# A long convolution feeding a two-layer block: channels in the array's stationary operand in the last transform step, and turns by VectorE in blocks of 32

## The chip, the cores and the metric

The kernel runs on one core of one Trainium2 chip. The metric is the device time of one execution in microseconds. The kernel before has a median of 3762.23 us over 3 runs (3761.11 to 3762.27). Traces and profile pages come from one profiled execution each. Engines are named as the profile names them: PE (TensorE matmul), PEld (its weight load), DVE (VectorE), ACT (ScalarE), POOL (GpSimd), and SP (SyncE), which issues almost all DMAs.

## What is computed

Two blocks, one after the other, in float32. The first is a convolution over the sequence by a filter that a small network makes; the second is applied to every row of its output.

```python
# batch 4, seq 12480, d_model 128
h_filt = (relu(pos_emb @ w1) @ w2) * exp(-0.01 * pos)     # (12480, 128)
u = x * v                                                  # (4, 12480, 128)
y = irfft(rfft(u, n=2*S) * rfft(h_filt, n=2*S))[:, :S, :]  # causal convolution by channel
a = (x * y).reshape(4 * 12480, 128)
h = a @ w_in                                               # w_in (128, 2048)
out = (h * cos(h)) @ w_out                                 # w_out (2048, 128)
```

## The kernel before

**The convolution** is a transform over 96 x 120 points in two steps forward and two back, all as matmuls. A position of the sequence is n1 x 120 + n2, with n1 from 0 to 103 (R = 104) and n2 from 0 to 119. The steps of one batch, with their lines:

- `u_units` loads x and v, multiplies them and forms sums and differences of mirrored rows in the big tile `slots` (`u_sums`, L401).
- `f1` (L407): for each channel, a stationary operand of 124 places of one channel, and a moving table of 192 columns. DVE and ACT take turns at moving the results into `parts`, which is a view of `slots` (`f1_evict`).
- `f2` (L448): for each pair of frequencies, a moving operand of all 128 channels. Its result is multiplied with the filter's transform `h`, which is loaded for each unit (`before` in `f2_units`, with `w`), in `f2_product` (DVE, then POOL L474).
- `i1` (L479): for each channel, a stationary operand of 96 places of one channel and a moving table of 120 columns; `i1_evict` (ACT L487, DVE L489) puts the result into `slots`.
- `i2` (L504), the last transform step: for each group g of four rows n2 (`n2s(g)`; 30 groups in a batch), eight matmuls. Stationary is a table `t` of 96 x 104, moving are the 128 channels of one place, so that the result has n1 on the partitions and the channels in the free dimension. `i2_out` multiplies by x (tile `xs`, one DMA a group by `load_pairs`, L376) into `zs` (L511) and stores `zs` to the DRAM tile `zd` (L517).

float32 matmuls run as two passes, so each matmul in the program is two in the profile.

`slots` is laid out as 64 pairs of channels, then places, then the 2 channels of a pair:

```python
slots = spool.tile([P, CB, 2 * N2, 2], F32, name="slots")
```

A channel's places are thus 8 bytes apart, and the channels of one place are 64 runs of 8 bytes.

**The layers** work on tiles of 128 rows of `zd` (the first has 104, the last 88; 98 in all), and every row holds the four n2 of its group, so a tile has up to 512 tokens. `moe_load` loads a tile, `moe_turn` turns it by four PE transposes (helper line L126) into PSUM, from where ACT copies it (L737) to `at`, with the channels on the partitions. Then 16 steps follow, one for each 128 hidden channels: `moe_up` (PE L743, ACT L746, DVE L749, POOL L752), `moe_act` (ACT L757, DVE L759) and, four steps later (`LAG`), `moe_down` (PE L768), which sums into the PSUM bank `acc`. There is one such bank; after the last convolution every second tile uses one of the convolution's banks instead. `moe_evict` (ACT L774) copies the sums, `moe_back` turns them back by four PE transposes and an ACT copy (L783), and `moe_store` (L794) writes them with one DMA for each piece of a group that lies in the tile, about two a tile.

**The order of the work** is written out by hand; no scheduler moves anything. The first batch's convolution runs almost alone; from its last transform step on, the layers' steps and the convolution of the next batches are interleaved: each layer step owes one unit, and `next(conv, ...)` runs pieces of the convolution that are worth it (`I2_STEPS` and its like). Every engine executes its instructions in this order, SP its DMAs too. DMAs count their completion on eight semaphores in turn, so a DMA may wait for the one eight before it. When the convolutions are done, only the layers run. `load(n + 2)` is called at step 12 of tile n.

Of the kernel before, what the change touches and what calls it, by code (L numbers as in the profile page):

```python
# [16 lines left out]
P = 128  # L17
# [13 lines left out]
def kernel(  # L31
# [74 lines left out]
    LAG = 4  # L106
    WCOL = 256

    dram = ctx.enter_context(tc.tile_pool(name="dram", bufs=1, space=DRAM))
    hd = dram.tile([N1 // 2, N2, 2, CB, 4], F32, name="hd")  # L110
    zd = dram.tile([NROWS, G, D], F32, name="zd")
# [241 lines left out]
    def filter_out(pool, bank, aT, slots, j, w2_sb):  # L353

        ps = bank()
        for i, jj in enumerate((j, H - 1 - j)):
            nc.tensor.matmul(ps[0:FR, i * 2 * D:(i + 1) * 2 * D], aT[:, jj, 0:FR],
                             w2_sb[:, :], start=True, stop=True)
        above = pool.tile([FR, 2, CB, 2], F32, name="above", bufs=2)
        pj = ps[0:FR, :].rearrange("p (n b i) -> p n b i", n=4, i=2)  # L360
        nc.scalar.copy(out=above[:, :, :, :], in_=pj[:, 2:4])
        a = H - 2 - 2 * j
        for place, op in ((a, ALU.add), (ODD + a, ALU.subtract)):
            nc.vector.tensor_tensor(
                slots[0:FR, :, place:place + 2, :].transpose([0, 2, 1, 3]),
                pj[:, 1::-1], above[:, :, :, :], op=op)
# [14 lines left out]
    def clear_gap(u):  # L381

        nc.gpsimd.memset(u[:, :, H:ODD, :], 0.0)
# [13 lines left out]
    def u_sums(u, tiles, a):  # L397
        both = tiles[0][:, :, :].rearrange("p h (n b i) -> p h n b i", n=UA, i=2)
        below, above = both[:, 0, ::-1, :, :], both[:, 1, :, :, :]
        for place, op, e in ((a, ALU.add, nc.gpsimd), (ODD + a, ALU.subtract, nc.vector)):  # L400
            e.tensor_tensor(u[0:R, :, place:place + UA, :].transpose([0, 2, 1, 3]),  # L401
                            below, above, op=op)


    def f1_mm(ps, u, b, i):

        nc.tensor.matmul(ps[0:KE, i * 2 * N1:(i + 1) * 2 * N1], u[:, b, 0:KE, i],  # L407
# [12 lines left out]
    def f1_evict(ps, b, share):  # L420
        copy, negated = f1_takers(b, share)
        pj = ps[:, 0:4 * N1].rearrange("p (i r k) -> p r k i", i=2, r=2)
        copy(out=parts[0:ODD, :, :, b, :], in_=pj[0:ODD])
        yield
        copy(out=parts[ODD:KE, 0, :, b, :], in_=pj[ODD:KE, 1])
        negated(parts[ODD:KE, 1, :, b, :], pj[ODD:KE, 0])
        yield

    def f1_evict_filter(ps, b, share):
# [3 lines left out]
        near, far = ftile[:, b, :, :], above[:, b, :, :]  # L433
# [8 lines left out]
    def f2_mm(ps, w, k1, i, filt=False):  # L442
# [3 lines left out]
        pi = ps[0:N2, :].rearrange("p (r b g i) -> p g r b i", r=2, g=2, i=2)[:, i]  # L446
        if not filt:
            nc.tensor.matmul(pi, w[:, i, :], parts[0:KE, :, k], start=True, stop=True)  # L448
        elif k < KF:
            both = ftile[0:KE, :, k:k + N1 + 1:N1, :].rearrange("p b r i -> p r b i")  # L450
            nc.tensor.matmul(pi, w[:, i, :], both, start=True, stop=True)
        else:
            for r, src in enumerate((ftile[0:KE, :, k, :], above[0:KE, :, k - KF, :])):
                nc.tensor.matmul(pi[:, r], w[:, i, :], src, start=True, stop=True)

    def f2_product(pool, ps, h, k1, whole):


        y = parts[0:N2, :, k1:k1 + 2, :, :].rearrange("p r k b i -> p r b (k i)")
        t = pool.tile([N2, 2, CB, 4], F32, name="t", bufs=1 + whole)  # L460
        uu = ps[0:N2, :].rearrange("p (r b j) -> p r b j", r=2, j=4)
        if whole:
            for r, (dst, hh) in enumerate(((y, h[:, :, :, :]), (t[:, :, :, :], h[:, ::-1, :, :]))):
# [13 lines left out]
    def i1_mm(ps, b, i):  # L477
        for r in range(2):
            nc.tensor.matmul(  # L479
                ps[0:N1, (i * 2 + r) * N2:(i * 2 + r + 1) * N2],  # L480
                parts[0:N2, r, :, b, i],
                cs[:, r, :], start=True, stop=True)

    def i1_evict(pool, ps, b):
# [3 lines left out]
        for h, op in ((0, ALU.add), (1, ALU.subtract)):  # L488
            nc.vector.tensor_tensor(slots[0:N1, b, h * N2:(h + 1) * N2, :], pj[:, 0],  # L489
                                    other[:, :, :], op=op)  # L490
            yield

    def i2_mm(ps, t, g, part):
        for i in range(part * G // 2, (part + 1) * G // 2):
# [8 lines left out]
            for r, place in enumerate(places):  # L503
                nc.tensor.matmul(ps[0:R, i * D:(i + 1) * D], t[:, i, r, :],  # L504
                                 slots[0:N1, :, place, :], start=(r == 0), stop=(r == 1))

    def i2_out(pool, ps, xs, b, g):
        if b == 0:
            yield
        zs = pool.tile([R, 2, UA, D], F32, name="zs")  # L510
        nc.vector.tensor_tensor(  # L511
            zs[:, :, :, :].rearrange("p h n d -> p (h n d)"), ps[0:R, :],
            xs[:, :, :].rearrange("p h n -> p (h n)"), op=ALU.mult)
        z = zs[:, :, :, :].rearrange("p h n d -> p (h n) d")
        row = (b * NG + g) * R
        if row > 0:
            nc.sync.dma_start(zd[row:row + R, :, :], z)  # L517
        else:
            zbs[0] = z
        made[0] += 1  # L520
        yield

    rows_psum = []
    made = [0]
    zbs = {}
# [65 lines left out]
    def f2_units(bank):  # L591
        with tc.tile_pool(name="there", bufs=3) as pool:
            ws, hs = {}, {}

            def before(j):
                ws[j] = pool.tile([KE, 2, N2], F32, name="w")
                nc.sync.dma_start(ws[j][:, :, :], wd[j, :, :, :])
                hs[j] = pool.tile([N2, 2, CB, 4], F32, name="h")
                nc.sync.dma_start(hs[j][:, :, :, :], hd[j, :, :, :, :])
# [10 lines left out]
    def f2_both_units(bank):  # L610

        with tc.tile_pool(name="both", bufs=2) as pool:
# [15 lines left out]
            def after(j, ps):  # L628
                h = pool.tile([N2, 2, CB, 4], F32, name="h", bufs=3)
                nc.scalar.activation(h[:, :, :, :].rearrange("p r b j -> p (r b j)"),  # L630
                                     ps[1][0:N2, :], AF.Copy, scale=1.0 / M)
                nc.sync.dma_start(hd[j, :, :, :, :], h[:, :, :, :])
# [32 lines left out]
    def i2_units(bank, b, bufs):  # L665

        with tc.tile_pool(name="back", bufs=2, side="left" if b else "right") as pool:
            ts, xss = {}, {}

            def before(j):  # L670
                ts[j] = pool.tile([N1, G, 2, R], F32, name="tm", bufs=bufs)
                xss[j] = pool.tile([R, 2, UA * D], F32, name="xs", bufs=bufs)
                load_pairs(xss[j], x, b, n2s(j)[0], n2s(j)[UA])
                if b == 0 and j not in SOME:
                    return make_group(pool, j, ts[j], 1)
                nc.sync.dma_start(ts[j][:, :, :, :], td[j, :, :, :, :])

            def mm(j, ps, i):
                if i == 0:
                    ps = bank()  # L680
                i2_mm(ps, ts[j], j, i)
# [3 lines left out]
                             lambda j, ps: i2_out(pool, ps, xss.pop(j), b, j),  # L685
                             4 if b == 0 else 2, ahead=bufs - 1, skip=int(b == 0))

    def inverse_units(bank, b):
# [6 lines left out]
        new = u_units(b + 1, 3, slots[0:R, :, :, :],  # L695
# [10 lines left out]
    def forward_units(bank, back):  # L706
# [3 lines left out]
        yield from f1_units(bank, slots[0:R, :, :, :])  # L710
# [13 lines left out]
    def moe_load(pool, n):  # L724
        m, row = rows_of(n), first_row(n)
        zb = pool.tile([P, G, D], F32, name="zb", bufs=2)
# [278 lines left out]
```

## Time and profile before

| | |
|---|---|
| median of 3 runs (lowest, highest) | 3762.23 us (3761.11, 3762.27) |
| span of the profiled execution, first to last instruction | 3758.9 us |
| the profiled execution's own time | not given apart; its span lies 3.3 us under the median of the runs |
| granted TensorE clock, mean | 0.995 |
| f1 of the four batches (L407), first the filter's | 64-166, 594-729, 1410-1541, 2232-2364 us |
| i2 of the four batches (L504) | 338-565, 1178-1383, 1992-2206, 2815-2946 us |
| layers alone | about 3000 us to the end |
| DMA issues on SP | 1341 |

A row of the profile's groups gives the line, the engine, what is written from what, partitions x elements, the count, then busy time and mean duration in ns, then the idle time of the engine before these instructions and what ended it. Idle time of an engine counts only where that engine, or someone who waits for it, is on the chain that ends last.

### The profile page before, as it was taken

The numbers are of one execution on the slowest core, as the hardware profiler recorded it, in microseconds if no ns is written. First come the engines' busy times: TensorE is split into PE (matmuls) and PEld (weight loads), VectorE is DVE, ScalarE is ACT, GpSimd is POOL, SyncE is SP. The second block draws the span as 40 slices with busy tenths as digits, with TensorE's granted clock in tenths as the row PEclk, the third lists the DMA queues.
The fourth block names the chain that finished last, engine by engine and source line by source line (L and its number), as shares of the span: only waits on it lengthen the run. The fifth ranks groups of instructions, "written<-read, shape, count | busy, mean of one in ns | idle before, by whom it ended". The sixth has DMA issues, their size and how long they took to land.

```text
span 3758.9 us, 47177 instructions
## 1 busy us (share of the span) xinstructions
PE 3690.6 (98%) x13546; PEld 2110.4 (56%) x13546; DVE 2773.7 (74%) x5586; ACT 2508.2 (67%) x4660; POOL 2557.6 (68%) x2318
## 2 busy tenths in 40 slices
PE   7898999999999999999999999999999999999999
PEld 6777555555566556555565556555566544444444
DVE  8887997687866787788766776788765666666666
ACT  5757776766665557766665567666664677777777
POOL 6666776588845665688745664788644677777776
PEclk9999999999999999999999999999999999999999
DMA  6263551022203650122104530122105200000000
GB/s 167 64 185 107 155 167 33 25 72 79 72 12 91 181 151 12 40 79 77 52 18 128 180 105 21 52 79 76 38 21 172 76 23 17 17 23 18 17 23 13
DMA packets 209499, 276.14 MB, mean 73 GB/s; under 512 B 17111, under 2 KB 146535, under 8 KB 209111
## 3 DMA queue, kind: packets, MB, share of 16 engines
q1 hardware_dynamic: 209239, 273.12, 24.8%
q8 instruction: 109, 1.79, 0.2%
q14 instruction: 151, 1.24, 0.1%
HBM read 193.64 MB, written 79.42 MB: 73 GB/s over the span
## 4 chain that ended last, share of the span: by engine, by line
PE 88%; DVE 3%; POOL 3%; ACT 2%; DMA 2%; issue 1%; SPq 0%; POOLq 0%; DVEq 0%; ACTq 0%
PE ph L743 33%; PE acc L768 28%; PE cv L504 5%; PE cv L768 5%; PE cv L479 4%; PE cv L407 3%; PE cv L448 3%; PE ph L126 2%; POOL f L752 1%; PE ps L407 1%; PE ps L448 1%; DMA tm<-td 1%; DMA wd<-w 1%; ACT cs L757 1%; DVE k L749 1%
## 5 line engine op out<-in xcount | busy, mean ns | idle before, releaser
L752 POOL TENSOR_TENSOR f<-a,k 128x512 f32<-128x512 f32 (+1 forms) x1568 | 1986.2, 1267 | 1060.5 <-DVE k L749 1059.1
L743 PE MATMUL ph<-at,w_in_sb 128*128 128x512 f32 (+1 forms) x3136 | 1599.0, 591 | 3.7 <-DVE gt L759 2.7
L746 ACT ACTIVATE a<-ph,quarter 128x512 f32<-128x512 f32 (+1 forms) x1568 | 1071.2, 683 | 704.8 <-PE ph L743 695.2
L768 PE MATMUL acc<-gt,w_out_sb 128*128 128x512 f32 (+1 forms) x2688 | 1370.3, 591 | 0.0
L759 DVE TENSOR_TENSOR gt<-ph,cs 128x512 f32<-128x512 f32 (+1 forms) x1568 | 1077.3, 687 | 359.9 <-ACT cs L757 341.8
L757 ACT ACTIVATE cs<-f 128x512 f32<-128x512 f32 (+1 forms) x1568 | 981.0, 626 | 366.6 <-POOL f L752 364.3
L749 DVE TENSOR_SCALAR k<-a 128x512 f32<-128x512 f32 (+1 forms) x1568 | 792.9, 506 | 550.7 <-ACT a L746 524.2
L768 PEld LDWEIGHTS acc<-gt,w_out_sb 128*128 128x128 f32 x2688 | 508.4, 189 | 642.8 <-issue 631.9
L743 PEld LDWEIGHTS ph<-at,w_in_sb 128*128 128x128 f32 x3136 | 553.2, 190 | 337.7 <-issue 257.5
L474 POOL TENSOR_TENSOR slots<-slots,t 120x256 f32<-120x256 f32 x384 | 312.9, 821 | 59.9 <-DVE t L467 25.6
L504 PEld LDWEIGHTS cv<-slots,tm 96*104 96x104 f32 x1920 | 238.6, 169 | 106.8 <-issue 85.4
L504 PE MATMUL cv<-slots,tm 96*104 96x128 f32 x1920 | 251.7, 273 | 9.9 <-POOL tm L297 5.0
L768 PE MATMUL cv<-gt,w_out_sb 128*128 128x512 f32 (+1 forms) x448 | 224.5, 583 | 1.0 <-DVE gt L759 1.0
L479 PEld LDWEIGHTS cv<-cs,slots 120*96 120x96 f32 x1536 | 176.7, 167 | 67.2 <-issue 65.2
L479 PE MATMUL cv<-cs,slots 120*96 120x120 f32 x1536 | 183.2, 266 | 0.0
L448 PEld LDWEIGHTS cv<-slots,w 124*120 124x120 f32 x576 | 103.7, 184 | 124.3 <-issue 112.3
L407 PEld LDWEIGHTS cv<-c,slots 104*124 104x124 f32 x768 | 132.6, 192 | 72.2 <-issue 60.0
L448 PE MATMUL cv<-slots,w 124*120 124x256 f32 x576 | 173.0, 380 | 0.0
L407 PE MATMUL cv<-c,slots 104*124 104x192 f32 x768 | 151.8, 327 | 5.4 <-DVE gt L759 3.5
L768 PEld LDWEIGHTS cv<-gt,w_out_sb 128*128 128x128 f32 x448 | 84.9, 190 | 104.8 <-issue 99.5
L489 DVE TENSOR_TENSOR slots<-cv,other 96x240 f32<-96x240 f32 x384 | 133.1, 394 | 1.5 <-ACT other L487 1.4
L395 DVE TENSOR_TENSOR xt<-xt,vt 104x256 f32<-104x256 f32 x177 | 132.6, 751 | 0.6 <-DMA vt<-in_v_dram 0.6
(131 smaller groups left out, 2520.9 us busy)
## 6 DMA issues: line engine op xcount, KB each, us to landing
h<-hd SPq DMA_DIRECT2D x144, 240.0 KB
tm<-td SPq DMA_DIRECT2D x96, 312.0 KB
xt<-in_x_dram SPq DMA_DIRECT2D x120, 208.0 KB
vt<-in_v_dram SPq DMA_DIRECT2D x120, 208.0 KB
xs<-in_x_dram SPq DMA_DIRECT2D x120, 208.0 KB
zd<-zs SPq DMA_DIRECT2D x119, 208.0 KB
zb<-zd SPq DMA_DIRECT2D x96, 256.0 KB
w<-wd SPq DMA_DIRECT2D x144, 116.2 KB
```

The costliest lines, as they stand in the source:

```text
L407: nc.tensor.matmul(ps[0:KE, i * 2 * N1:(i + 1) * 2 * N1], u[:, b, 0:KE, i], c1[0:u.shape[0], :, :].rearrange("p r k -> p (r k)"), start=Tr ...
L448: nc.tensor.matmul(pi, w[:, i, :], parts[0:KE, :, k], start=True, stop=True)
L474: nc.gpsimd.tensor_tensor(y[:, r], y[:, r], t[:, r], op=op)
L479: nc.tensor.matmul(ps[0:N1, (i * 2 + r) * N2:(i * 2 + r + 1) * N2], parts[0:N2, r, :, b, i], cs[:, r, :], start=True, stop=True)
L504: nc.tensor.matmul(ps[0:R, i * D:(i + 1) * D], t[:, i, r, :], slots[0:N1, :, place, :], start=(r == 0), stop=(r == 1))
L743: nc.tensor.matmul(ph[:, 0:m], w_in_sb[:, c * P:(c + 1) * P], ats[n][:, 0:m], start=True, stop=True)
L746: nc.scalar.activation(a[:, 0:m], ph[:, 0:m], AF.Identity, bias=quarter[:, 0:1], scale=INV_TWO_PI)
L749: nc.vector.tensor_scalar(out=k[:, 0:m], in0=a[:, 0:m], scalar1=ROUND, scalar2=ROUND, op0=ALU.add, op1=ALU.subtract)
L752: nc.gpsimd.tensor_tensor(f[:, 0:m], a[:, 0:m], k[:, 0:m], op=ALU.subtract)
L757: nc.scalar.activation(cs[:, 0:m], f[:, 0:m], AF.Sin, scale=TWO_PI)
L759: nc.vector.tensor_tensor(gt[:, 0:m], ph[:, 0:m], cs[:, 0:m], op=ALU.mult)
L768: nc.tensor.matmul(accs[n][:, 0:m], w_out_sb[:, c, :], gt[:, 0:m], start=(c == 0), stop=(c == NFC - 1))
```

## The change

`slots` becomes places, then 128 channels: a channel's places are now 512 bytes apart, and the channels of one place are contiguous. Every reader and writer of `slots`, `parts`, `above`, `ftile` and `h` follows. In the last transform step the operands change places: the channels of a place are stationary (96 x 128) and the table moves (104 columns), so the result has the channels on the partitions. For that x has to be there with its channels on the partitions: it is loaded in blocks of 32 channels, 16 DMAs a group (`blocks_load`), and turned by one VectorE transpose of 32 x 32 blocks (`blocks_turn`), called for the next group after each product. `zd` holds channels by rows, the layers' tile is loaded as it is used, and `moe_turn` goes. On the way out VectorE turns the sums from PSUM in blocks of 32 (`moe_evict`), `moe_back` goes, and `moe_store` writes runs of 32 channels, 16 DMAs for each piece; the last tile's go half from ACT's queue. The load of a tile is called at step 2 of the tile before it.

The core of the diff:

```diff
+    SQ = 32
+    ROWB = SQ // G
+    NB = R // ROWB
...
-    zd = dram.tile([NROWS, G, D], F32, name="zd")
+    zd = dram.tile([B * NG, D, G, R], F32, name="zd")
...
-        nc.tensor.matmul(ps[0:KE, i * 2 * N1:(i + 1) * 2 * N1], u[:, b, 0:KE, i],
+        nc.tensor.matmul(ps[0:KE, i * 2 * N1:(i + 1) * 2 * N1], u[:, 0:KE, 2 * b + i],
...
-                parts[0:N2, r, :, b, i],
+                parts[0:N2, r, :, 2 * b + i],
...
-                nc.tensor.matmul(ps[0:R, i * D:(i + 1) * D], t[:, i, r, :],
-                                 slots[0:N1, :, place, :], start=(r == 0), stop=(r == 1))
-
-    def i2_out(pool, ps, xs, b, g):
+                nc.tensor.matmul(ps[0:D, i * R:(i + 1) * R], slots[0:N1, place, :],
+                                 t[:, i, r, :], start=(r == 0), stop=(r == 1))
+
+    def blocks_load(t, b, g):
+
+        for i, n2 in enumerate(n2s(g)):
+            for a in range(D // SQ):
+                start = x[b, n2, a * SQ:(a + 1) * SQ]
+                first = a * SQ + i * ROWB
+                nc.sync.dma_start(
+                    t[first:first + ROWB, :, :],
+                    bass.AP(tensor=start.tensor, offset=start.offset,
+                            ap=[[N2 * D, ROWB], [ROWB * N2 * D, NB], [1, SQ]]))
+
+    def blocks_turn(pool, t):
+
+        xt = pool.tile([D, G, R], F32, name="xt", bufs=2)
+        nc.vector.transpose(
+            xt[:, :, :].rearrange("d i (n r) -> d n i r", r=ROWB),
+            t[:, :, :].rearrange("p n (i r) -> p n i r", r=ROWB))
+        return xt
...
+                    xbs[j] = pool.tile([P, NB, SQ], F32, name="xb", bufs=3)
+                    blocks_load(xbs[j], b, j)
...
-        zb = pool.tile([P, G, D], F32, name="zb", bufs=2)
-        nc.sync.dma_start(zb[0:m, :, :], zd[row:row + m, :, :])
...
+            nc.sync.dma_start(to[:, :, done:done + rows], zd[group, :, :, n1:n1 + rows])
...
-        ot = pool.tile([D, BANK], F32, name="ot", bufs=1)
-        nc.scalar.copy(out=ot[:, 0:m], in_=accs.pop(n)[:, 0:m])
+        ot = pool.tile([P, BANK // SQ, SQ], F32, name="ot", bufs=2)
+        nc.vector.transpose(
+            ot[:, 0:m // ROWB, :],
+            accs.pop(n)[:, 0:G * m].rearrange("d (i n r) -> d n i r", i=G, r=ROWB))
...
+            for i, n2 in enumerate(n2s(g)):
+                for a in range(D // SQ):
...
+                    issuers[a % 2].dma_start(
...
-            slots = spool.tile([P, CB, 2 * N2, 2], F32, name="slots")
+            slots = spool.tile([P, 2 * N2, D], F32, name="slots")
...
-                if c == NFC - 4 and n + 2 < NALL:
-                    load(n + 2)
+                if c == 2 and 0 < n < NALL - 1:
+                    load(n + 1)
```

## The prediction

> **What bounds the kernel now.** I read the page first (engine shares, the granted clock, the chain), then the PE timeline for what one piece of work costs in PE time, then SyncE's own queue, because the change turns few large DMAs into many small ones.
>
> ```profile
> PE 3690.6 (98%) x13546; PEld 2110.4 (56%) x13546; DVE 2773.7 (74%) x5586; ACT 2508.2 (67%) x4660; POOL 2557.6 (68%) x2318
> ...
> PEclk9999999999999999999999999999999999999999
> ...
> PE 88%; DVE 3%; POOL 3%; ACT 2%; DMA 2%; issue 1%; SPq 0%; POOLq 0%; DVEq 0%; ACTq 0%
> ```
>
> TensorE sets the time: 98% busy at a clock granted in full (mean 0.995), 88% of the chain. No other engine is above 74%, and SP's queue is no part of the chain. So PE work that goes is time gained, as long as nothing else becomes later than PE.
>
> A matmul's row (273 ns, 592 ns) contains latency that overlaps the next one, so I take PE time from starts. From the PE timeline of the last stage, where only the layers run:
>
> ```profile
> 3205.22 1.02 PE L768 MATMUL acc<-gt,w_out_sb 128*128 128x512 f32 x2
> 3206.08 0.60 PE L126 MATMUL ph<-ident,ot 128*128 128x128 f32 x4
> 3206.52 1.02 PE L743 MATMUL ph<-at,w_in_sb 128*128 128x512 f32 x2
> ```
>
> Four transposes hold PE from 3206.08 to 3206.52, 0.436 us with more digits (109 ns each); a layer matmul of 512 columns takes 0.858 us in its two passes.
>
> SP's queue in the last transform step of the second batch, about one group of four rows n2 (start, duration):
>
> ```profile
> 1201.16 0.31 SPq L376 DMA_DIRECT2D xs<-in_x_dram  x1
> 1201.57 0.34 SPq L676 DMA_DIRECT2D tm<-td  x1
> 1201.95 0.39 SPq L517 DMA_DIRECT2D zd<-zs  x1
> 1202.45 0.33 SPq L376 DMA_DIRECT2D xt<-in_x_dram  x1
> 1205.47 0.33 SPq L376 DMA_DIRECT2D vt<-in_v_dram  x1
> 1207.76 0.31 SPq L376 DMA_DIRECT2D xs<-in_x_dram  x1
> ```
>
> Five issues in 6.6 us. An issue takes 0.31 to 0.39 us and the next follows 0.05 us later. How fast the groups come is in the rows of their last product (L511), one answer for each batch:
>
> ```profile
> L511 DVE TENSOR_TENSOR zs<-cv,xs x30: 673/680/690, 341.9 to 568.9; 104x512 f32<-104x512 f32 x30
> ...
> L511 DVE TENSOR_TENSOR zs<-cv,xs x30: 678/680/690, 1179.6 to 1386.5; 104x512 f32<-104x512 f32 x30
> ...
> L511 DVE TENSOR_TENSOR zs<-cv,xs x30: 678/680/682, 2000.3 to 2209.4; 104x512 f32<-104x512 f32 x30
> ...
> L511 DVE TENSOR_TENSOR zs<-cv,xs x30: 678/680/681, 2821.1 to 2948.7; 104x512 f32<-104x512 f32 x30
> ```
>
> Over 29 intervals that is 7.83, 7.13, 7.21 and 4.40 us a group. These four stages are where the change puts its load.
>
> **Removed from PE.** The turns of the layers' input and output: 98 tiles x 8 transposes, 196 fours x 0.436 = 85.5 us. They save nothing in the four stages if these come to run at another pace (below): some 20 of the 98 tiles lie there, so 78 x 0.872 = 68 us count. ACT loses the three copies around them, 98 x (0.574 + 0.574 + 0.584) = 170 us; ACT waits for PE 695 us already, so 0.
>
> **The last step's matmuls.** 1920 passes, now 128 stationary and 104 moving columns instead of 104 and 128. Eight start 0.111 us apart today; by moving columns alone 104/128 x 107 + 2 = 89 ns, but two 128-column weight loads never start closer than 108 ns. Gain between 0 and 42 us; I take 0, since these passes lie in the four stages. The moving operand of L448 becomes contiguous: 218 to 223 ns falls towards the 216 of L357, some 4 ns x 576 = 2 us gained.
>
> **Added to DVE.** 120 turns of x (416 elements): between 471 ns (L749 at 416) and 586 (L759 at 416, one operand from PSUM); 98 turns out of PSUM (512): between 574 (the ACT copy) and 690 (L759). I take the upper rows, 70 + 68 us, less 120 x (680 - 586) = 11 for the smaller product. DVE goes from 2774 to 2901 us and stays off the path. The fullest place is the first batch's stage, 205.7 of 227 us busy today, +19. If a turn cost twice, DVE would still fill less than the time that SP needs there. On the path is only the accumulator: one bank, freed by DVE now behind a k (0.43) and its own 0.69, where ACT took 0.58; up to 0.3 us in the 70 tiles that do not alternate banks, I take 6 us in all.
>
> **Added to SP.** This decides. A group's x was one DMA and becomes 16 (4 rows x 4 blocks of channels, each 8 x 13 runs of 128 B); a tile's output was about 2 and becomes about 34; the tile's load becomes about 2. SP issues in order. In the changed program's order on SP, from the third block load of a batch to the last, I count 691, 740, 756 and 554 issues, over 28, 28, 28 and 27 groups (per group 16 + tm + zd, mostly + xt + vt, and the stores of the tiles that run beside). The price of an issue: 308 + 51 ns for xs then zd, 377 ns from one output store to the next (66 pairs). I take 0.365 us. Shortest start-to-start in the trace: 0.286 (w then h); longest ordinary one: 0.417 (output stores whose own row is 0.367).
> - Batch 0: 691 x 0.365 = 252 us, 28 x 7.83 = 219 today: +33
> - Batch 1: 270, 200 today: +70
> - Batch 2: 276, 202 today: +74
> - Batch 3: 202, 27 x 4.40 = 119 today: +83
>
> Together +260 us (+94 at 0.30, +403 at 0.417). Nothing covers it: DVE's turn of the next group waits for its 16 loads, and DVE is in order, so the k and gate products queued behind it wait too, and with them POOL, ACT and, four steps later, PE. The three buffers give about two groups of lead, not 28.
>
> Elsewhere the stores have room (34 x 0.365 = 12.4 us of 28 to 45 us a tile), but they come in one burst ahead of others' loads. In the second transform step w and h for two units ahead (6.2 us each) queue behind it: about 12 us of burst against 12.4 us of lead less the load's own time. 0 to 4 us for each of 22 tiles; I take 2, so 44 us. The load of the next tile moves to step 2 of the tile before, at least 14 x 1.72 = 24 us ahead: 0. The end: the last copy, transposes and copy (0.45 + 0.65 + 0.58 us) become one turn of 0.5 us, but one store becomes 16 over two queues: +2.
>
> **Stationary operands at 512-byte steps.** f1 (L407) and i1 (L479) now read one channel of [place, channel], where they read every second float. No row has such a step. The nearest:
>
> ```profile
> L743 PEld LDWEIGHTS ph<-at,w_in_sb 128*128 128x128 f32 x3136 | 553.2, 190 | 337.7 <-issue 257.5 <-DVE gt L759 26.7 <-ACT at L737 17.0
> ...
> L479 PEld LDWEIGHTS cv<-cs,slots 120*96 120x96 f32 x1536 | 176.7, 167 | 67.2 <-issue 65.2 <-PE ph L743 1.9
> ...
> L357 PEld LDWEIGHTS ps<-w_sb,slots 128*96 128x96 f32 x120 | 19.5, 163 | 7.7 <-POOL slots L401 1.5
> ```
>
> At 8-byte steps 96 columns take 167 ns, contiguous 163: free. The 32 columns between 163 and 190 give 0.83 ns a column, so 80 ns for i1 and 103 for f1, under matmuls that start 102 and 162 ns apart. Bounds: 0, or a doubled column part, 160 and 206, which passes the matmul by 58 and 44: 2048 x 58 + 1280 x 44 = 175 us, about 165 as the first f1 is not PE's. I take 0, the nearest row, and keep 165 as a rival.
>
> [...]
>
> **Sum.** 3758.9 + 260 - 68 - 2 + 6 + 44 + 2 = 4001 us of span; the median of the runs lies 3.3 us above this profile's span, so about **4000 us**.
>
> **Rivals.**
> - SP keeps up, and PE's gain stands. That needs 200/740 = 0.27 us an issue in batch 1 and 0.21 in batch 3; the sum breaks even near 0.28 us. For it: SP is idle most of the time today, and the loads of w take only 0.24. Against: the xs row itself. All 85 us are kept: 3677 us.
> - SP binds as above and the strided weight loads double too: 4000 + 165 = 4165. For it: PE has no slack in those stages, 98%. Against: the 8-byte rows.
> - The DMA engines bind, not the issue: a group's 208 packets of 1 KB become 1664 of 128 B. If one costs what the trace's 512-byte packets cost (34 ns) and only eight engines share them, 7 us a group, beside the other 6: 13 us against SP's 9.7, 3.3 x 120 = 400 us more: 4400.
>
> **Chances.** Forecast 0.50, with the doubled loads 0.35, DMA engines 0.07, SP keeps up 0.08. Low end: issues at 0.30 and no trouble from the bursts, 3790. High end: doubled loads with issues at 0.40 (+96), about 4260. About 0.2% either way (7.5 us) is what a measurement can tell from no change; only the keep-up case or a mix with it comes out there or below: faster 0.08, same 0.01, slower 0.91.
>
> **What would show it.** Right: in the four stages SP issues back to back, DVE waits for xb, groups come 9 to 10 us apart (7.5 in batch 3), PE falls to about 75% there, and tiles in the last stage take 27.5 us instead of 28.3. Wrong: groups at today's pace (an issue is cheaper than its row); L479 passes more than 102 ns apart or loads well over 167 ns (steps cost); stages much longer with SP waiting for DMAs (packets); a granted clock below 0.99 in the new gaps would add to any of these.

## The result and the profile after

The changed kernel takes **4507.11 us** (median of 4 runs, 4505.10 to 4510.67), against 3761.71 for the kernel before on the same chip: 1.198 times as long, 95% interval 1.196 to 1.200. The profiled execution's span is 4504.1 us. The forecast was 4000 with a range of 3790 to 4260, so the sign was right, the size was not, and the time lies outside the range.

The page of the changed kernel, in the order in which that of before was shown: busy time, granted clock in 40 slices, and the chain of waits by engine.

```profile
PE 3965.8 (88%) x12762; PEld 2316.2 (51%) x12762; DVE 2832.8 (63%) x5804; ACT 2387.1 (53%) x4366; POOL 2539.3 (56%) x2316
...
PEclk9998989999998889999999888999999889999999
...
PE 62%; DMA 12%; SPq 11%; DVE 5%; POOL 4%; issue 4%; ACT 2%; DVEq 0%; POOLq 0%
```

PE runs 784 passes fewer and yet is busy 275 us longer. 91 us of that are also there in the version with one load and one store below, at a clock of 0.994: the layout's longer passes less the turns that are gone. The other 184 go with the granted clock (mean 0.934; before 0.995): in the last step's four stages it is 0.81 to 0.87, where the row shows an 8, in the second step's three later ones 0.92 to 0.94. DMA and SP's queue, 2% and 0% of the chain before, are now 23%.

The last step's product (L535, before L511) in batches 1, 2 and 3, one answer each:

```profile
L535 DVE TENSOR_TENSOR zs<-cv,xt x29: 574/581/583, 1391.7 to 1713.4; 128x416 f32<-128x416 f32 x29
...
L535 DVE TENSOR_TENSOR zs<-cv,xt x29: 573/580/583, 2434.3 to 2763.9; 128x416 f32<-128x416 f32 x29
...
L535 DVE TENSOR_TENSOR zs<-cv,xt x29: 580/592/593, 3474.9 to 3701.4; 128x416 f32<-128x416 f32 x29
```

Over 28 intervals that is 11.5, 11.8 and 8.1 us a group, where before it was 7.1, 7.2 and 4.4 and the forecast was 9 to 10 (7.5 in the last). What PE and DVE wait for, from the table of waits (total us, times, longest):

```profile
PE cv L507 <- DMA tm<-td: 275.0, 57, 19.2
...
DVE zs L535 <- DMA zd<-zs: 145.0, 28, 16.9
PE cv L451 <- DMA w<-wd: 129.8, 24, 9.6
```

The wait that was forecast, VectorE's for x, hardly exists (6.0 us). PE waits for the table `tm` of the last step and for the weights `w` of the second; VectorE waits for a free `zs`, almost only in the last batch (136 of the 145 us). SP's queue and PE's timeline at the longest kind of wait (start, duration, count; the idle time before in brackets):

```profile
1492.05 11.77 SPq L824 DMA_DIRECT2D out_dram<-ot  x32
1503.91 0.33 SPq L708 DMA_DIRECT2D tm<-td  x1
1504.28 6.38 SPq L516 DMA_DIRECT2D xb<-in_x_dram  x16
```

```profile
1507.57 2.01 PE L507 MATMUL cv<-tm,slots 96*128 96x104 f32 x8 [12.87 <-DMA tm<-td]
1509.37 1.95 PE L778 MATMUL ph<-at,w_in_sb 128*128 128x512 f32 x2
1511.12 1.77 PE L803 MATMUL acc<-gt,w_out_sb 128*128 128x512 f32 x2
1512.72 1.03 PE L507 MATMUL cv<-tm,slots 96*128 96x104 f32 x8
```

A tile's 32 stores hold SP for 11.8 us; `tm` is queued behind them and issued at 1503.91; PE, in order, stands still for 12.9 us, and its first work afterwards takes twice as long (2.01 us for eight passes that take 1.03 a little later).

The stationary operands at 512-byte steps (before: 167 and 192 ns for the same groups):

```profile
L482 PEld LDWEIGHTS cv<-cs,slots 120*96 120x96 f32 x1536 | 277.4, 255 | 65.5 <-issue 65.5
...
L409 PEld LDWEIGHTS cv<-c,slots 104*124 104x124 f32 x768 | 187.5, 300 | 66.8 <-issue 34.7
```

So there are three candidates: the strided loads, the number of issues on SP, and the order in which SP takes them.

### The profile page after: what moved, and what is told of

Read it like the earlier page. It is cut to its first block, busy times and chain, and to the rows that moved or that the text cites. A ratio compares the mean times of both kernels' runs of the same rounds, so it can differ in the third digit from the quotient of the medians.

```text
span 4504.1 us, 50834 instructions
## 1 busy us (share of the span) xinstructions
PE 3965.8 (88%) x12762; PEld 2316.2 (51%) x12762; DVE 2832.8 (63%) x5804; ACT 2387.1 (53%) x4366; POOL 2539.3 (56%) x2316
## 4 chain that ended last, share of the span: by engine, by line
PE 62%; DMA 12%; SPq 11%; DVE 5%; POOL 4%; issue 4%; ACT 2%; DVEq 0%; POOLq 0%
PE ph L778 22%; PE acc L803 17%; SPq L824 8%; PE cv L482 5%; DMA tm<-td 5%; PE cv L803 4%; PE cv L409 3%; PE cv L507 3%; POOL f L787 2%; SPq L516 2%; DMA w<-wd 2%; PE ps L482 2%; DMA xb<-in_x_dram 2%; PE cv L451 2%; DMA vt<-in_v_dram 2%
## 5 line engine op out<-in xcount | busy, mean ns | idle before, releaser
L778 PE MATMUL ph<-at,w_in_sb 128*128 128x512 f32 (+1 forms) x3136 | 1674.4, 616 | 34.9 <-DVE gt L794 34.6
L803 PE MATMUL acc<-gt,w_out_sb 128*128 128x512 f32 (+1 forms) x2688 | 1425.7, 613 | 28.2 <-DVE ot L809 28.1
L784 DVE TENSOR_SCALAR k<-a 128x512 f32<-128x512 f32 (+1 forms) x1568 | 752.6, 480 | 1095.9 <-ACT a L781 1080.1
L778 PEld LDWEIGHTS ph<-at,w_in_sb 128*128 128x128 f32 x3136 | 589.2, 200 | 423.1 <-issue 317.8
L507 PE MATMUL cv<-tm,slots 96*128 96x104 f32 x1920 | 294.7, 305 | 290.8 <-DMA tm<-td 275.0
L507 PEld LDWEIGHTS cv<-tm,slots 96*128 96x128 f32 x1920 | 286.1, 220 | 436.0 <-issue 301.8
L482 PEld LDWEIGHTS cv<-cs,slots 120*96 120x96 f32 x1536 | 277.4, 255 | 65.5 <-issue 65.5
L482 PE MATMUL cv<-cs,slots 120*96 120x120 f32 x1536 | 269.3, 322 | 0.0
L409 PEld LDWEIGHTS cv<-c,slots 104*124 104x124 f32 x768 | 187.5, 300 | 66.8 <-issue 34.7
L535 DVE TENSOR_TENSOR zs<-cv,xt 128x416 f32<-128x416 f32 x119 | 69.2, 582 | 148.9 <-DMA zd<-zs 145.0
```

What stands on the lines that cost most here:

```text
L482: nc.tensor.matmul(ps[0:N1, (i * 2 + r) * N2:(i * 2 + r + 1) * N2], parts[0:N2, r, :, 2 * b + i], cs[:, r, :], start=True, stop=True)
L507: nc.tensor.matmul(ps[0:D, i * R:(i + 1) * R], slots[0:N1, place, :], t[:, i, r, :], start=(r == 0), stop=(r == 1))
L778: nc.tensor.matmul(ph[:, 0:m], w_in_sb[:, c * P:(c + 1) * P], ats[n][:, 0:m], start=True, stop=True)
L784: nc.vector.tensor_scalar(out=k[:, 0:m], in0=a[:, 0:m], scalar1=ROUND, scalar2=ROUND, op0=ALU.add, op1=ALU.subtract)
L803: nc.tensor.matmul(accs[n][:, 0:m], w_out_sb[:, c, :], gt[:, 0:m], start=(c == 0), stop=(c == NFC - 1))
```

## The experiments: dividing the loss

Stage lengths below run from the first to the last matmul start of a stage, summed over all its runs in the program, as read from the traces; "end" is from PE's last matmul to the end of the span.

**The layout alone.** The kernel before, with `slots` as places, then channels; its loads, transposes and stores are kept.

```diff
-            slots = spool.tile([P, CB, 2 * N2, 2], F32, name="slots")
+            slots = spool.tile([P, 2 * N2, D], F32, name="slots")
...
-        nc.tensor.matmul(ps[0:KE, i * 2 * N1:(i + 1) * 2 * N1], u[:, b, 0:KE, i],
+        nc.tensor.matmul(ps[0:KE, i * 2 * N1:(i + 1) * 2 * N1], u[:, 0:KE, 2 * b + i],
```

> The kernel before with the new layout of slots (places, then channels) and nothing else: the last step keeps its operands, its one load of x a group, the PE transposes and the two stores a tile. Theory A (a stationary operand at 512-byte steps loads its columns at half the rate): i1 passes 165 ns apart instead of 102, f1 213 instead of 162, weight loads 255 and 300 ns; 2048 x 63 + 768 x 51 + about 8 in the first f1 = 176 us, so 3762 + 176 = about 3935 us. Theory B (the slow loads in the changed kernel are a consequence of its low clock or of the many DMAs, not of the step): 102 and 162 ns as before, 3755 to 3765 us.

Measured: 3904.16 us, ratio 1.038 (1.036 to 1.039). The strided loads cost 143 us of span. The same two groups in this kernel:

```profile
L478 PEld LDWEIGHTS cv<-cs,slots 120*96 120x96 f32 x1536 | 276.1, 255 | 57.3 <-issue 55.2
...
L405 PEld LDWEIGHTS cv<-c,slots 104*124 104x124 f32 x768 | 185.3, 300 | 57.4 <-issue 27.8
```

The first theory has the mechanism (its loads of 255 and 300 ns), the second is out; its 3935 was 31 us too high. i1 grows from 490 to 602 us and f1 from 500 to 537; f2 (955) and i2 (778) stay. A few us of the 149 come back elsewhere. PE shows it directly. Eight passes of i1 in the kernel before, then eight in this one:

```profile
1095.38 0.98 PE L479 MATMUL cv<-cs,slots 120*96 120x120 f32 x8
1096.21 1.03 PE L743 MATMUL ph<-at,w_in_sb 128*128 128x512 f32 x2
```

```profile
1130.32 1.42 PE L478 MATMUL cv<-cs,slots 120*96 120x120 f32 x8
1131.57 1.03 PE L742 MATMUL ph<-at,w_in_sb 128*128 128x512 f32 x2
```

From the first start to the next group's it is 0.83 us against 1.25: the passes follow the loads now, not the matmuls. In such a group of eight the first pass takes 107 ns as before, the second 156 and the others 165 (before: 102). In the same groups of the changed kernel, whose passes have the same three spacings, the first load starts 0.43 us before its pass, under the layers' matmul ahead of it; the loads after it start 0.145 and then 0.165 us apart (medians of 75 groups). That is why the theory's 165 for all of them was too much.

**Each kind of small DMA alone, and neither.** Three versions of the changed kernel: x by one load a group, output by one store a piece, and both. The load and the store then move the same bytes, but in contiguous runs of a partition, so x is read and the output written in another order.

```diff
-        for i, n2 in enumerate(n2s(g)):          # x: 16 loads
-            for a in range(D // SQ):
...
+        nc.sync.dma_start(t[:, :, :], bass.AP(... ap=[[NB * SQ, P], [1, NB * SQ]]))
...
-            for i, n2 in enumerate(n2s(g)):      # output: 16 stores
-                for a in range(D // SQ):
...
+            nc.sync.dma_start(bass.AP(... ap=[[count * G, P], [1, count * G]]),
+                              ot[:, at:at + count // ROWB, :])
```

One load of x, 16 stores:

> The changed kernel with x loaded by one DMA a group instead of 16 (the same bytes in rows of 1664 B; the values then belong to other places, so the product is with other values of x). Theory A (the number of issues on SP in the last step is what costs): the four stages of that step return from 310, 336, 340, 238 us to about 230 to 260, 220 to 250, 220 to 250, 130 to 160, as only the stores' bursts are left on SP; total about 4110 to 4180. The second step keeps its 336 to 351 us. Theory B (the stores' bursts alone do it): the stages lose less than 30 us each, total above 4380.

16 loads of x, one store:

> The changed kernel with one store for each piece of a tile's output instead of 16 (the same bytes in longer runs, written to other places of the output). Theory A: the second step returns from 336 to 351 us to about 287 each, -172 in all; the last step's stages have 21 issues a group left, 7.6 us, and fall to about 235, 230, 235, 205; total about 4010 to 4060. Theory B (the loads alone fill SP): the last step's stages stay above 300 us, total about 4300.

Both one:

> The changed kernel with one load of x a group and one store a piece (both leave the order of the values out). Theory A (SP's issues and the strided weight loads are the whole story): clock back at 0.99, all stages of the last step and of the second step at or under their times before, and what is left is the strided loads less the transposes: 3762 + 176 - 85 = about 3850 us. Theory B (something else in the change costs too, such as VectorE's turns, the accumulator freed later, or the shorter lead of the tile loads): above 3900 us.

Measured: 4184.02 (one run), 4126.15 (one run) and 3858.27 us (ratio 1.026, 1.024 to 1.028). The first lies 4 us above its first theory. The second fits neither of its theories: f2 is back as the first says, but the last step's stages are 276, 280, 277 and 214 us where it asked for 235, 230, 235 and 205, so an issue costs more than its 0.36 us. The third fits its first theory.

| kernel | span | f2 | i1 | i2 | end |
|---|---|---|---|---|---|
| before | 3758.9 | 957 | 490 | 778 | 4.0 |
| layout alone | 3901.6 | 955 | 602 | 778 | 4.0 |
| one load, one store | 3854.2 | 954 | 589 | 776 | 3.5 |
| one load, 16 stores | 4182.1 | 1128 | 588 | 913 | 20.5 |
| 16 loads, one store | 4124.4 | 952 | 588 | 1046 | 3.5 |
| changed kernel | 4504.1 | 1128 | 588 | 1223 | 20.8 |

The second and third rows differ by the turns and the swapped last step: 47 us less. The third and the last differ by the small DMAs: 650 us, of which 447 are in i2, 174 in f2 and 17 at the end. f2 and the end are the stores' doing alone. In i2 the loads cost 270, the stores 137, and both together 447.

Why 47 and not the 64 of the forecast (68 + 2 - 6)? PE's busy time falls from 3851.6 to 3781.7 us, by 70. But its idle time (gaps between matmuls in the trace) rises from 41 to 64. A wait that the layout alone does not have is that of a new sum for the bank that VectorE turns:

```profile
PE acc L800 <- DVE ot L806: 32.5, 37, 2.7
```

The forecast had 6 us for this wait. It is more than the whole rise of 23, so other idle time fell; no run took this wait away by itself.

## The experiments: what SP's queue does

**Stores spread.** Changed kernel; the stores are taken four to a layer step from step 4 on, instead of all at step 8.

```diff
+                    yield                      # after each store
...
-                if c == NFC // 2 and n - 1 in ots:
-                    moe_store(n - 1, ots.pop(n - 1))
+                if c == LAG and n - 1 in ots:
+                    storing[0] = moe_store(n - 1, ots.pop(n - 1))
+                for _ in range(4):
+                    next(storing[0], None)
```

> The changed kernel, with the stores of a tile's output issued four to a layer step instead of all in one burst; the number of issues is the same. Theory A (it is the burst that hurts: the loads of w, h and of the table tm queue behind 32 stores, about 12 us): the second step's three later stages go from 336/351/344 back to about 290 us each (-160 us together), the last step's stages lose the part of their 1223 us that lies above SP's issue time (about 1000 us), perhaps half of it (-110): 4200 to 4300 us. Theory B (the count of issues alone decides, a burst or not): the last step's stages stay within 20 us of 1223 and the second step's within 20 us of 1031: 4480 to 4520 us.

Measured: 4296.39 us, ratio 1.142 (1.141 to 1.144). f2 is back at 953 us: the burst theory holds there entirely. In i2 it does not: 1194 instead of 1223, 29 us of the 110 that it asked for. The total lies in its range all the same, because f2 gave 15 us more than forecast and the range was wide. Windows of the second step's three later stages, the changed kernel and then this one (busy time of PE, PEld, DVE, ACT, POOL, granted clock, DMA share, GB/s):

```profile
863.00:1199.00 336.00, 297.31 (x743) 145.38 (x742) 232.44 (x471) 177.08 (x277) 248.57 (x232) 0.94 0.27 63
1891.00:2242.00 351.00, 302.27 (x744) 147.01 (x744) 231.28 (x472) 176.61 (x277) 247.05 (x231) 0.92 0.26 62
2943.00:3287.00 344.00, 297.29 (x744) 145.22 (x743) 233.19 (x471) 176.72 (x277) 248.20 (x232) 0.93 0.26 62
```

```profile
855.00:1139.00 284.00, 280.66 (x745) 138.91 (x744) 237.54 (x470) 177.90 (x276) 247.84 (x231) 1.00 0.31 76
1813.00:2101.00 288.00, 280.72 (x745) 138.74 (x744) 235.32 (x469) 178.12 (x277) 247.41 (x231) 1.00 0.30 74
2786.00:3070.00 284.00, 280.47 (x744) 138.80 (x743) 238.20 (x470) 177.01 (x277) 248.14 (x231) 1.00 0.30 74
```

The same matmuls take 897 us of PE in the first and 842 in the second. So the burst cost 175 us: 120 of PE standing still (1031 - 897 against 856 - 842), and 55 of work at the lower clock after each stand.

**The table from ACT's queue.** Changed kernel, one line.

```diff
-                    nc.sync.dma_start(ts[j][:, :, :, :], td[j, :, :, :, :])
+                    nc.scalar.dma_start(ts[j][:, :, :, :], td[j, :, :, :, :])
```

> The changed kernel, with only the load of the table tm issued from ACT's queue instead of SP's; SP has one issue less for each group, all others are as they were. Theory A (PE waits for tm, which stands on SP behind a burst of stores and 16 block loads, and the granted clock halves after such a wait): the last step's four stages, 1223 us, come down towards SP's issue time of about 1000 us, so 4300 to 4400 us, with the granted clock above 0.90 in them and no wait of PE for tm above 5 us; the second step's stages stay at 336/351/344. Theory B (SP's rate of issue sets these stages, and tm is only the load that happens to come last): PE then waits for another load instead, the stages fall by at most the issues taken away (115 x 0.36 = 41 us): 4460 to 4510 us.

Measured: 4726.06 us, ratio 1.257 (1.255 to 1.259): slower than either theory, i2 at 1444 us. PE no longer waits long for `tm`, but the wait has moved, as batch 1's stage shows:

```profile
DVE zs L535 <- DMA zd<-zs: 186.1, 25, 21.3
...
PE ph L778 <- DVE gt L794: 149.4, 21, 22.1
```

PE now runs into the next group; VectorE's product then needs a `zs` whose store waits its turn on SP among the loads of x, and in VectorE's order everything of the layers waits behind it. Why this is dearer than the wait at `tm` stands in the view of SP's own waits in this stage:

```profile
SPq L516 <- DMA tm<-td: 121.3, 24, 14.8
```

The load of `tm` still takes its turn on the same eight completion semaphores, so the DMA eight places behind it, a load of x on SP, waits until it has landed. ACT issues `tm` late: at 1610.77 us, for example, 2.0 us after a wait of 7.67 us for POOL has ended. Over the four stages SP held for 411 us, 320 of them for `tm`; in the changed kernel it is 148 in all. These 263 us more, less 88 issues fewer, are about the 221 us by which i2 grew. So the table's delay only moved to SP, by way of the semaphores.

**16 loads of large packets.** Changed kernel; a group's 16 loads read runs of 1664 bytes instead of 128.

```diff
-                            ap=[[N2 * D, ROWB], [ROWB * N2 * D, NB], [1, SQ]]))
+                        ap=[[NB * SQ, ROWB], [1, NB * SQ]]))
```

> The changed kernel, whose 16 loads of x for each group stay 16, but each reads runs of 1664 contiguous bytes instead of 104 runs of 128 bytes (so it takes other values of x). The issues are the same in number and in place; only the packets are fewer. In the changed kernel an issue takes 0.36 us from start to start in the middle case, but the last step's stages divided by their issues give 0.41 to 0.46 us, because SP pauses for 0.2 to 1.5 us at the sixth to ninth of a group's 16 loads. Theory A (issues bind, and the pauses come from the many small packets not yet moved): the pauses go and the four stages fall from 1223 towards 2795 x 0.365 = 1020 us, 4300 to 4400 us in all. Theory B (pauses come with the count of DMAs alone, whatever their packets): within 30 us of 4507. Theory C (small packets, not issues, make the stages long): they come back to about 910 us as with one load for a group, about 4180.

Measured: 4443.14 us, ratio 1.182 (1.180 to 1.183), i2 1162. Between the first two theories, and far from the third: 13 times larger packets on the loads are worth 61 us of 447 (the loads alone had cost 270). The pauses on SP largely stay (123 us where the changed kernel has 148), so most of them do not come from small packets. The rest goes with the number of DMAs, not with the size of the loads' packets; the stores kept their small packets here.

What SP does in i2 can now be read from its records. In the changed kernel's four stages it issues 2795 DMAs in 1224 us. In the middle case one starts 0.360 us after the other, as forecast (0.365), which would make 1006 us. There are 253 pauses of 0.15 us or more, together 148 us; the other 70 are issues that took longer than the middle one. Among the 16 loads of a group the pauses fall on the sixth to ninth, and the view of SP's waits (batch 1's stage) lays most of them to the large loads issued just before:

```profile
SPq L516 <- DMA tm<-td: 20.9, 26, 1.4
SPq L516 <- DMA vt<-in_v_dram: 14.1, 18, 1.3
```

They are fewest where such loads are missing: 18 us in the last batch (no x and v for a next one) and 22 in the first (most tables made on the spot), against 52 and 55 in the two between. The trace also says what SP holds for. In 224 of the 253 pauses (131 of the 148 us) it waits for its own DMA's completion semaphore, and what releases it is the landing of the DMA eight issues before, mostly `tm` (64 us) or `vt` (38). With eight semaphores in turn, the loads of x in the middle of a group come up behind `tm`, `xt` and `vt`. No run had another number of semaphores.

**Groups further apart.** Stores spread as above, and 5.5, 5.5, 5.5 and 4.5 layer steps for a group in the four batches, instead of 3.5, 3.0, 3.0 and 1.5.

```diff
-    U_STEPS, F1_STEPS, F2_STEPS, I1_STEPS, I2_STEPS = 2.0, 0.8, 2.9, 0.8, 1.5
-    FIRST_STEPS, I2U_STEPS = 3.5, 3.0
+    U_STEPS, F1_STEPS, F2_STEPS, I1_STEPS, I2_STEPS = 2.0, 0.8, 2.9, 0.8, 4.5
+    FIRST_STEPS, I2U_STEPS = 5.5, 5.5
```

> The changed kernel with the stores issued four to a layer step (as in the run with spread stores) and with the last step's groups set further apart among the layers' steps: 5.5 steps of the layers for a group instead of 3.5 in the first batch and 3.0 in the next two, 4.5 instead of 1.5 in the last. Work and issues are the same. Theory A (SP's issue time is a cost only because the groups are laid closer together than SP can feed them): PE fills the waits with layers' work it would else do after the last stage; the stages stay at 310 to 340 us, their clock comes back to above 0.97, the time after the last stage shrinks by the same amount, and what is left is the kernel with one load and one store (3858) and some 20 to 100 us more: 3870 to 3960 us. Theory B (the many small DMAs cost PE, the loads or the clock something that pacing can't hide): 4100 to 4300 us.

Measured: 4065.08 us, ratio 1.081 (1.080 to 1.083), between the two theories. 231 of the 438 us that spread stores still lost against one load and one store came back by order alone. The stages grew to 1428 us in all, above the 310 to 340 each of the first theory, because the layers brought along have stores too (3434 issues), and SP is full again. Batch 1's stage, the changed kernel and then this one:

```profile
1383.00:1719.00 336.00, 239.26 (x833) 135.62 (x832) 171.06 (x322) 110.46 (x178) 130.06 (x116) 0.84 0.46 108
```

```profile
1298.00:1678.00 380.00, 345.36 (x1101) 180.78 (x1102) 246.70 (x458) 196.78 (x310) 214.01 (x181) 0.94 0.43 101
```

PE is busy 345 of 380 us, where the changed kernel has 239 of 336. The cost of issues is therefore in large part where they stand, not that they are made.

## The experiments: the output's turn alone

These keep the layout, the loads and the input's transposes of the kernel before, and turn only the sums by VectorE. First with one store a piece (again in another order of the output), then with 16, four to a layer step:

```diff
-        nc.scalar.copy(out=ot[:, 0:m], in_=accs.pop(n)[:, 0:m])
+        nc.vector.transpose(ot[:, 0:m // ROWB, :],
+            accs.pop(n)[:, 0:G * m].rearrange("d (i n r) -> d n i r", i=G, r=ROWB))
...
-    def moe_back(pool, n, ot):                 # four PE transposes, an ACT copy
```

> As the run before it, but each piece goes out in one DMA of runs as long as a partition's data, so that it lands in another order in the output; SP has the old number of issues. It shows what the turn on VectorE alone is worth. Theory A: 3762 - 43 + up to 10 for the accumulator that is freed later = 3715 to 3735 us, and the run with spread stores lies within 10 us of it. Theory B (the turn delays the accumulator more than the transposes cost): 3760 us or more. If the run with spread stores is more than 20 us above this one, the stores cost even when spread.

> The kernel before (its layout, and its loads of x with TensorE's transposes of them, kept), with only the layers' output turned by VectorE and stored in 16 DMAs of 128-byte runs for each piece, four to a layer step. TensorE loses 98 fours of transposes x 0.436 = 43 us. Theory A (the loss of the change is in strided weight loads, x's loads and bursts; spread stores find room on SP): 3715 to 3740 us, faster than the kernel before. Theory B (any kernel with some 32 stores for a tile pays on SP in the second and last step): the second step's stages lose 20 us and more each, 3780 to 3900 us.

Measured: 3730.73 us (ratio 0.992, 0.991 to 0.994) and 3782.09 (1.007, 1.005 to 1.008). The turn is worth 30 us, as the first theory of its run has it; 16 stores cost 51 even when spread: i2 811 against 771, the end 15.3 against 3.5. That is the second theory of the other run, though only the two middle stages lose some 20 us each.

Then every second store from ACT's queue, and that with 4.0 and 3.75 layer steps a group instead of 3.5 and 3.0 in the first three batches:

```diff
-        row, issuers = first_row(n), [nc.sync, nc.scalar if n + 1 == NALL else nc.sync]
+        row, issuers = first_row(n), [nc.sync, nc.scalar]
...
-    FIRST_STEPS, I2U_STEPS = 3.5, 3.0
+    FIRST_STEPS, I2U_STEPS = 4.0, 3.75          # second of the two only
```

> The kernel before with only the layers' output turned by VectorE and stored in runs of 128 bytes, four stores to a layer step, and now every second store issued from ACT's queue instead of SP's. With all on SP it took 3782 us, 51 us more than with one store for a piece (3731), and 39 us of these stand in the last step's stages. Theory A (stores ahead of the table tm on SP delay PE's next group): the stages give back half or more of the 39 us and ACT, 65% busy, takes 17 issues a tile without delaying the layers: 3735 to 3765 us. Theory B (ACT, in order, delays the sines by its issues): 3790 us or more.

> The kernel before with only the output turned by VectorE, its stores four to a layer step over SP's and ACT's queues (3767 us), and with the last step's groups of the first three batches set further apart: 4.0 layer steps for a group instead of 3.5 in the first batch, 3.75 instead of 3.0 in the next two. The run with one store for a piece took 3731; of the 36 us between the two, 27 stand in the last step's first three stages, where PE waits for the table. Theory A (PE's waits for the table are only a matter of spacing): PE does layers' work in that time, and the 27 us come back: 3735 to 3750 us, below the kernel before's 3761. Theory B (the stores cost PE something that spacing doesn't hide, or the layers run out of rows): 3760 us or more.

Measured: 3767.05 and 3767.49 us (both 1.002, interval 1.001 to 1.003). Two queues give 15 of the 51 us back, a little less than the first theory asked. Wider spacing gives nothing more; here the second theory stands, and with two queues this spacing brings back none of the 36 us that remain. A row of waits of the last of these names the stores as what ACT's activations now wait for, 186 times:

```profile
ACT a L748 <- DMA out_dram<-ot: 80.3, 186, 2.4
```

Last, the 66 tiles whose sums end outside i2's stages turned by VectorE, four stores to a step on SP; the others, and the last tile, as before.

```diff
+        if not last_step[0] and n + 1 < NALL:
+            turned.add(n)
+            nc.vector.transpose(
```

> The kernel before, in which only those 66 tiles whose sums are complete outside the last transform step's stages are turned by VectorE and stored in runs of 128 bytes (four stores to a layer step); the tiles that end in the last step's stages, and the very last tile, keep TensorE's transposes and one store for a piece. TensorE loses 66 x 0.436 = 29 us. Theory A (the many stores cost only where SP or its order is short: the last step's stages, +39 us with all stores on SP, and the end, +12 us): 3733 to 3748 us, below the kernel before's 3761 and below the 3767 and 3782 of the runs with the turn in all tiles. Theory B (the many stores cost PE time wherever they stand, as the unchanged time of the run with wider spacing may mean): 3755 us or more.

Measured: **3745.62 us, ratio 0.996 (0.995 to 0.997)**, the first theory, and 14 us (0.4%) faster than the kernel before, measured beside it. i2 is at 780 us and the end at 3.9. The same turn with one store a piece gave 30 us in 98 tiles, which would be 21 in 66; so 16 stores a piece cost little where SP has nothing urgent behind them. 14 of the 29 us of PE work come back as time: PE's busy time fell by 22 us and its idle time rose by 9, with this wait in it:

```profile
PE acc L773 <- DVE ot L783: 7.0, 16, 0.8
```

## Why the prediction was right or wrong

| step of the sum | forecast | measured | by |
|---|---|---|---|
| strided weight loads | 0 | +143 | layout alone |
| PE's turns, L448, the accumulator | -64 | -47 | one load and store against layout alone |
| bursts in the second step | +44 | +174 | spread stores take all of it back |
| SP in the last step | +260 | +447 | with and without small DMAs |
| the end | +2 | +17 | the same |

These add up to 734 of the 745 us between the spans.

- **The step that failed in kind** is "I take 0, the nearest row" for the strided loads. The row at 8-byte steps was near in kind but not in step, and the upper bound (an estimate: a doubled column part, 160 and 206 ns of columns) was the right size: it made the loads 80 and 103 ns longer, and they became 88 and 108 longer (255 and 300). As time it gave 143 us where the rival had 165, since the layers' matmul ahead of each group of passes covers its first load (passes 107, 156, then 165 ns apart).
- **SP in the last step**: mechanism right, size short. The issue's price was right in the middle case (0.360 us against 0.365), and so was the count (2741 forecast, 2795 in the stages). What failed is to take the middle case for the mean: SP's pauses (148 us, 131 of them for the landing of the DMA eight before) and its longer issues (70 us) were not in the price, and 0.41 to 0.46 us a DMA came out. This is the largest miss, 187 us. Its upper price in the forecast, 0.417, would have given +403.
- **The bursts**: right mechanism, wrong lead. The forecast let a burst of 12 us meet up to 12 us of lead, 0 to 4 us a tile. The number of tiles was right (22 forecast, 24 stands of PE for `w`), the 2 us for each became 7: in batch 1's stage PE waited 38.4 us in 8 stands for `w`, 4.8 each, and lost about half as much again to the clock, which the forecast named but did not price.
- **The wait's place** was wrong: not VectorE for `xb` (6.0 us in all), but PE for `tm` (275 us), which is queued on the same SP behind stores and loads; the forecast did not follow `tm`.
- **The accumulator**: 6 us forecast for the sums that VectorE frees later; with one load and one store PE stood 32.5 us for it. That is 26 us more, where 17 are missing from the gain of 64.
- **The end**: after PE's last matmul 46 stores were still to be issued from SP, 16.1 us.
- **Right**: VectorE's turns took 600 and 711 ns against 586 and 690; the last step's swapped matmuls are no faster (776 against 778 us of i2); layer steps take 1.72 us, 27.5 us a tile, when alone.
- **The rivals**: "SP keeps up" is out by the start-to-start times. "The DMA engines bind" is out: larger packets on the loads are worth 61 us, and a packet of 128 bytes took 13 ns in the middle case, not the 34 that the rival took. "Doubled loads" was right as far as it went; the time needed it and the underpriced queue at once, so even its 4165 with the range's upper 4260 fell short.

## What to carry to other kernels

Count what a small DMA is queued in front of, not only its issue time: on an in-order queue the bursts of 32 stores cost nothing where only the layers ran (27.5 us a tile with them and without), and 175 us where the loads of the second step stood behind them. Price a saturated queue by its mean with the pauses in, here 20% above the middle case, and ask what large transfer stands eight places ahead on the same completion semaphore (131 of SP's 148 us of pauses here). For a stationary operand, look at the step between its columns before costing it at zero: 8 bytes was free here (96 columns in 167 ns, 163 contiguous), 512 doubled the column part of the load (255 ns in all), and no step between was run.

## What the runs showed of the hardware

- A float32 weight load at 512-byte steps between columns took 255 ns (96 columns) and 300 ns (124), against 167 and 192 at 8-byte steps: by the 0.83 ns a column of the rows before, the column part went from 80 to 168 ns and from 103 to 211.
- An issue on SP took 0.36 us from start to start in the middle case of the last step's stages, where most of the 2795 DMAs move up to 13 KB in runs of 128 bytes; the stages' length over their issues is 0.41 to 0.46 us.
- SP's pauses in the last step's stages were waits for the landing of the DMA eight issues before, on the same of eight semaphores, in 224 of 253 cases (131 of 148 us). A DMA moved to ACT's queue kept its place among these semaphores and held SP for 320 us in the four stages (121.3 in batch 1's).
- In the changed kernel, from the start of the first i2 stage to the end of the last, 74 of 88 waits of PE of 1.5 us or more were followed within 4 us by half the granted clock (512-column passes 0.6 to 0.9 us apart instead of 0.43), and none of 23 shorter ones (0.3 us and more). The half clock lasted until 3.0 to 6.8 us after the wait.
